# Loading q in rows of 1 KB and undoing the order where the outputs leave PSUM, in a retention and feed-forward kernel

## The chip, the cores and the metric

The kernel runs on one core of a Trainium2 chip. A core has a matrix engine (TensorE, PE in the profile) that writes its results to PSUM, eight banks of 512 fp32 values per partition; VectorE (DVE), ScalarE (ACT) and GpSimd (POOL) for elementwise work; SyncE (SP), which here issues transfers; and 16 DMA engines that carry them. PEld is TensorE's loading of weights. The metric is device time in microseconds (us) from the first to the last instruction. The kernel before takes 291.41 us, the median of three runs (291.38 to 291.48).

## What is computed

```python
# q, k, v: (8 batches, 8 heads, 576 tokens, 64), fp32
scores = scale * np.matmul(q, k.transpose(0, 1, 3, 2))
gamma = 1.0 - 2.0 ** (-5.0 - np.arange(H, dtype=np.float32))
Dmat = np.where(rel >= 0, gamma[:, None, None] ** rel[None, :, :], 0.0)   # rel = pos[:, None] - pos[None, :]
x = np.matmul(scores * Dmat[None], v)         # then heads side by side: (4608 tokens, 512)
h = np.maximum(x @ w_in, 0.0)                 # w_in: 512 x 2048
out = (h * h) @ w_out                         # w_out: 2048 x 512, out: (4608, 512) fp32
```

The first half is retention: attention without a softmax, with a decay per head. It can be computed in blocks of 64 tokens with a running state per head, and the kernel does so. The second half is a feed-forward layer with squared ReLU.

## The kernel before

The tokens are cut into 36 units: 32 "full" units of 128 tokens of one batch, and 4 "tail" units that join the last 64 tokens of two batches. The first 8 units go a way of their own ("paired"; not touched by the new load). Two units make a group, 18 in all. A unit's k, q and v are loaded as fp32, a partition per token, cast to fp16 by GpSimd (which also sorts the heads), and k and q are transposed by a DMA, so that the head dimension lies on the partitions. TensorE then forms, in quarters of its array (64 x 64, "quads"), the scores (psc), the sums of k and v for the state (psS) and the outputs (psO). VectorE masks the scores into rT, updates the state, and multiplies the outputs by powers of gamma while it moves them into xT, the input of the feed-forward matmuls ph (x by w_in) and po (by w_out; from the third group on, the second one in Strassen's seven products, whose sums are gS).

The order of instructions on each engine is not written down. Tasks with a modelled duration in us are handed to a list scheduler, and the program is emitted in the order that its simulation gives.

Loads, casts and transposes:

```python
    def dma_task(key, dur, fn, **kw):
        t = add("SP", key, dur, fn, deps=list(last_load), **kw)
        last_load[:] = [t]
        return t
# ...
    def add_load(u):
        kind, b, c = units[u]
        for n, (name, src) in enumerate((("k", k), ("q", q), ("v", v))):
            def fn(name=name, src=src):
                x = ld.tile([P, H, D], FP32, name=f"{name}32", tag=f"{name}32")
                tile_of[name + "32", u] = x
                if kind == "full":
                    nc.sync.dma_start(out=x, in_=src[b, :, c * P:(c + 1) * P, :].rearrange("h p d -> p h d"))
                else:
                    for i in range(2):
                        nc.sync.dma_start(out=x[i * 64:(i + 1) * 64],
                                          in_=src[b + i, :, 512:576, :].rearrange("h p d -> p h d"))
            loaded[name, u] = dma_task(0, 1.2 if loaded else 2.1, fn, acq=("ld",) if n == 0 else ())
# ...
        def sorted_cast(op, out_, in_):
            op(out=out_.rearrange("p (n b a d) -> p n b a d", n=2, b=2, a=2),
               in_=in_.rearrange("p (n a b) d -> p n b a d", n=2, a=2))

        def fk():
            t = tile_of["kq", u] = cast.tile([P, 2, H * D], FP16, name="kq16", tag="kq16")
            sorted_cast(nc.gpsimd.tensor_copy, t[:, 0], tile_of["k32", u])

        def fq():
            sorted_cast(nc.gpsimd.tensor_copy, tile_of["kq", u][:, 1], tile_of["q32", u])
# ...
        ck = add("POOL", base, 0.65, fk, deps=[loaded["k", u]], acq=("kq",))
        cq = add("POOL", base + 1, 0.62, fq, deps=[loaded["q", u], ck])
        cv = add("POOL", base + 2, 1.1, fv, deps=[loaded["v", u]] + tail, acq=("v16",))
# ...
        def fx2():
            t = tile_of["kqT", u] = work.tile([P, 2 * NP, P], FP16, name="kqT", tag="kqT", bufs=6)
            nc.sync.dma_start_transpose(out=t, in_=tile_of["kq", u].rearrange("p x n -> p (x n)"))
        T["kqT", u] = [add("SP", -1, 2.7, fx2, deps=[ck, cq], acq=("kqT",), after=3.0, lag=LAG_T)]
```

Here a row of q that a transfer moves is one token of one head, 64 fp32 values or 256 B. Scores, and the products of q with the state:

```python
    def emit_scores(g):

        tile_of["psc", g] = banks("psc")
        for s, u in enumerate(units_of(g)):
            kT = tile_of["kqT", u]
            ps = [x[:, cols(s)].rearrange("p (n i) -> p n i", i=64) for x in tile_of["psc", g]]
            for hp in range(NP):
                for a, c in ((0, 0), (1, 1), (0, 1), (1, 0)):
                    quad(ps[a][half(c), hp, :], kT[half(a), hp, half(c)], kT[half(a), NP + hp, half(c)], a, c)
# ...
    def put(g, u, c, h, lhsT, rhs, row):
        col = h % 2
        s = units_of(g).index(u)
        quad(tile_of["psO", g][c][half(col), 256 * s + 64 * (h // 2):256 * s + 64 * (h // 2) + 64], lhsT, rhs, row, col,
             start=(g, c, col) not in begun)
        begun.add((g, c, col))

    def inter(g, u, other):
        st = states(u)
        for n in range(2):
            for a, b in ((0, 0), (1, 1), (0, 1), (1, 0)):
                c = a ^ other
                if c in st:
                    x = 2 * n + b
                    put(g, u, c, 4 * n + 2 * a + b, tile_of[st[c][:2]][half(a), st[c][2], half(x)],
                        tile_of["kqT", u][half(a), NP + x, half(c)], a)

# ...
```

The masks, the eviction of the scores and the eviction of the outputs (add takes engine, priority, modelled us, what to emit; "ff" are the eight PSUM banks):

```python
    mask = const.tile([P, 64], FP32, name="mask")
    nc.gpsimd.memset(mask, 1.0)
    for c in range(2):
        nc.gpsimd.affine_select(out=mask[c * 64:(c + 1) * 64], in_=mask[c * 64:(c + 1) * 64],
                                compare_op=ALU.is_ge, fill=0.0, base=0, pattern=[[1, 64]], channel_multiplier=-1)
# ...
    def after_scores(g, t, key):
        for a in range(2):
            def fm(a=a):
                if a == 0:
                    tile_of["rT", g] = work.tile([P, 2, 2, NP, 64], FP16, name="rT", tag="rT", bufs=2)
                tile_of["masking", g] = nc.vector.tensor_tensor(
                    out=tile_of["rT", g][:, :, a],
                    in0=tile_of["psc", g][a].rearrange("p (s n i) -> p s n i", s=2, i=64),
                    in1=mask.rearrange("p (o r i) -> p o r i", o=1, r=1).to_broadcast([P, 2, NP, 64]), op=ALU.mult)
            m = add("DVE", key + a, 0.7, fm, deps=[t] + (T["masked", g][-1:] if a else []), acq=() if a else ("rT",))
            sched.free("ff", [m])
            T.setdefault(("masked", g), []).append(m)
        sched.free("prS", [m])
# ...
        for c in range(2):
            def fx(c=c):
                if c == 0:
                    tile_of["x", g] = x_pool.tile([P, NP, n * P], FP16, name="xT", tag="xT")
                nc.vector.tensor_tensor(
                    out=tile_of["x", g].rearrange("p n (s c i) -> p c s n i", s=n, c=2)[:, c],
                    in0=tile_of["psO", g][c].rearrange("p (s n i) -> p s n i", s=n, i=64),
                    in1=gam[units[us[0]][0]][:, c].rearrange("p (s n) i -> p s n i", s=1).to_broadcast([P, n, NP, 64]), op=ALU.mult)
            x = add("DVE", key + 0.1 * c, 0.7, fx, deps=[t2] + ([x] if c else []), acq=() if c else ("x",))
            sched.free("ff", [x])
        for u in us:
            T["x", u] = x
        sched.free("prO", [x])
```

The score matmuls of the next group and the output matmuls of the current one are emitted together from group 7 on.

## Time and profile before

| | us | share of the span |
|---|---|---|
| span of the profiled execution | 289.7 | |
| TensorE busy | 281.1 | 97% |
| ScalarE busy | 188.7 | 65% |
| VectorE busy | 181.2 | 63% |
| GpSimd busy | 85.8 | 30% |
| hardware DMA queue of SyncE: 134,848 packets, 44.84 MB | | 74.2% of 16 engines |

The profile is one execution. In its first part each engine's busy time is given; in the second the span is cut into 40 slices, and a digit is the busy share of a slice in tenths (9 is 90% or more). A row of the costliest groups names the line of the kernel, the engine, the operation, what it writes and reads ("out<-in"), then the shapes (partitions x elements and type), the count, the busy time in us and the mean ns of one instruction, and last the idle time of the engine just before these instructions with what ended it. A row of DMA issues gives the issuing engine's queue (SPq), the count, KB each, and the us from issue to landing. Matmuls are pipelined, so the durations of single ones overlap, and the end of a matmul is modelled.

### The profile page before, as it was taken

To read this page: it belongs to the slowest core of one execution; us is meant where nothing else is said; L and a number is where in the kernel's file an instruction comes from. 1 tells how busy PE (TensorE), PEld (TensorE's weight loads), DVE (VectorE), ACT (ScalarE), POOL (GpSimd) and SP (SyncE) were. 2 spreads that over 40 slices of the span, in tenths; PEclk is the share of its full clock that TensorE was granted. 3 is DMA by queue.
4 is the path that set the end of the run, shared out by engine and by line. 5 is a ranking of instruction groups with operands and counts; after the bars stand their busy time and mean duration, and the time that the engine had idled before them with its cause. 6 is when DMAs were issued, how large, how long until landed. Compare 5 with 4: busy or idle time off the path is not lost.

```text
span 289.7 us, 9992 instructions
## 1 busy us (share of the span) xinstructions
PE 281.1 (97%) x4322; PEld 233.3 (81%) x4322; DVE 181.2 (63%) x381; ACT 188.7 (65%) x361; POOL 85.8 (30%) x121
## 2 busy tenths in 40 slices
PE   7899999998999999999999999999999999999994
PEld 2568755787888888888888888888888888888883
DVE  3772369668585758736866757675777675455632
ACT  6459964684767676767767657586767676747830
POOL 5660035444434342342605151506240500000000
PEclk9999999999999999999999999999999999999998
DMA  7999999999899799999759699999994820201004
GB/s 197 276 208 205 249 289 256 183 228 210 186 185 211 158 225 198 214 223 231 149 147 211 139 226 198 180 190 211 226 179 140 186 83 2 75 2 72 2 6 141
DMA packets 139436, 49.94 MB, mean 172 GB/s; under 512 B 118144, under 2 KB 135040, under 8 KB 139392
## 3 DMA queue, kind: packets, MB, share of 16 engines
q1 hardware_dynamic: 134848, 44.84, 74.2%
q0 software_dynamic: 4224, 4.19, 8.8%
q8 instruction: 34, 0.56, 0.8%
q10 hardware_dynamic: 320, 0.26, 0.4%
q14 instruction: 10, 0.08, 0.1%
HBM read 36.70 MB, written 9.44 MB: 159 GB/s over the span
## 4 chain that ended last, share of the span: by engine, by line
PE 75%; DVE 1%; issue 0%; DVEq 0%
PE ph L853 36%; PE po L945 33%; PE psO L346 3%; PE psS L346 1%; PE psc L346 1%; DVE o L968 0%; DVE rT L673 0%; DVE p L997 0%; DVEq L968 0%
## 5 line engine op out<-in xcount | busy, mean ns | idle before, releaser
L853 PE MATMUL ph<-xT,w_in 128*128 128x256 f16 x1152 | 139.7, 273 | 0.1
L853 PEld LDWEIGHTS <-w_in 128*128 128x128 f16 x1152 | 110.9, 98 | 14.8 <-DMA w_in<-in_moe_w_in_dram 0.4
L861 ACT ACTIVATE rl<-ph 128x512 f16<-128x512 f32 x144 | 84.6, 588 | 49.6 <-PE ph L853 48.0
L871 ACT ACTIVATE gT<-rl 128x512 f16<-128x512 f16 x118 | 74.4, 631 | 3.4
L945 PEld LDWEIGHTS <-gS 128*128 128x128 f16 x512 | 49.5, 98 | 6.0
L945 PE MATMUL po<-wT,gS 128*128 128x256 f16 x384 | 51.9, 273 | 0.0
L922 DVE TENSOR_TENSOR gS<-gT,gS 128x512 f16<-128x512 f16 x64 | 32.5, 513 | 15.1 <-ACT gT L871 14.5
L945 PEld LDWEIGHTS <-gT 128*128 128x128 f16 x384 | 37.2, 98 | 5.3 <-issue 0.9
L922 DVE TENSOR_TENSOR gS<-gT 128x512 f16<-128x512 f16 x64 | 30.4, 477 | 15.7 <-ACT gT L871 15.6
L360 POOL CAST kq<-k 128x512 f16<-128x512 f32 x28 | 19.0, 679 | 63.8 <-DMA k<-in_k_dram 59.8
L945 PE MATMUL po<-w_out,gT 128*128 128x256 f16 x256 | 34.7, 273 | 0.7 <-DVE rT L673 0.7
L372 POOL TENSOR_TENSOR v<-v,vdec_full 128x512 f16<-128x512 f32 x24 | 26.6, 1107 | 20.2 <-DMA v<-in_v_dram 16.9
L360 POOL CAST kq<-q 128x512 f16<-128x512 f32 x28 | 18.5, 661 | 29.9 <-DMA q<-in_q_dram 29.7
L958 ACT COPY u<-po 128x256 f32<-128x256 f32 x32 | 11.8, 368 | 19.8 <-PE po L945 19.7
L968 DVE TENSOR_TENSOR o<-po,u 128x256 f32<-128x256 f32 x31 | 13.0, 420 | 16.0 <-PE po L945 9.3
L729 DVE TENSOR_TENSOR xT<-psO,gam_full 128x512 f16<-128x512 f32 x28 | 18.1, 685 | 6.5 <-PE psO L346 6.4
L873 DVE TENSOR_TENSOR gT<-rl 128x512 f16<-128x512 f16 x26 | 13.4, 517 | 12.4 <-ACT rl L861 11.9
L673 DVE TENSOR_TENSOR rT<-psc,mask 128x512 f16<-128x512 f32 x28 | 18.3, 683 | 3.4 <-PE psc L346 3.4
L968 DVE TENSOR_TENSOR o<-po,p 128x256 f32<-128x256 f32 x17 | 7.2, 423 | 16.7 <-ACT u L958 10.9
L945 PE MATMUL po<-w_out,gS 128*128 128x256 f16 x128 | 17.3, 273 | 0.0
L945 PE MATMUL po<-wT,gT 128*128 128x256 f16 x128 | 16.6, 273 | 0.0
L893 PE MATMUL po<-w_out,gT 128*128 128x512 f16 x64 | 15.8, 380 | 0.0
(78 smaller groups left out, 220.8 us busy)
## 6 DMA issues: line engine op xcount, KB each, us to landing
out_dram<-o SPq DMA_DIRECT2D x32, 256.0 KB, 3.5
k<-in_k_dram SPq DMA_DIRECT2D x24, 256.0 KB, 4.5
q<-in_q_dram SPq DMA_DIRECT2D x24, 256.0 KB, 5.1
v<-in_v_dram SPq DMA_DIRECT2D x24, 256.0 KB, 4.9
pair<-in_k_dram SPq DMA_DIRECT2D x4, 512.0 KB, 7.0
pair<-in_q_dram SPq DMA_DIRECT2D x4, 512.0 KB, 7.3
pair<-in_v_dram SPq DMA_DIRECT2D x4, 512.0 KB, 7.1
w_in<-in_moe_w_in_dram POOLq DMA_DIRECT2D x4, 512.0 KB, 8.9
```

The source lines that it names most:

```text
L346: t = nc.tensor.matmul(out_, lhsT=lhsT, rhs=rhs, start=start, stop=True, skip_group_check=True, tile_position=(64 * row, 64 * col))
L360: op(out=out_.rearrange("p (n b a d) -> p n b a d", n=2, b=2, a=2), in_=in_.rearrange("p (n a b) d -> p n b a d", n=2, a=2))
L372: nc.gpsimd.tensor_tensor(out=t, in0=tile_of["v32", u], in1=vdec[kind].rearrange("p (h o) -> p h o", o=1).to_broadcast([P, H, D]), op=ALU. ...
L673: tile_of["masking", g] = nc.vector.tensor_tensor(out=tile_of["rT", g][:, :, a], in0=tile_of["psc", g][a].rearrange("p (s n i) -> p s n i" ...
L729: nc.vector.tensor_tensor(out=tile_of["x", g].rearrange("p n (s c i) -> p c s n i", s=n, c=2)[:, c], in0=tile_of["psO", g][c].rearrange("p ...
L853: nc.tensor.matmul(tile_of["ph", g, fb][:, j, :], lhsT=w_in16[:, m, fi * P:(fi + 1) * P], rhs=tile_of["x", g][:, m, :], start=(m == 0), st ...
L861: nc.scalar.activation(out=t, in_=tile_of["ph", g, fb], func=ACTF.Relu)
L871: nc.scalar.activation(out=t, in_=rl, func=ACTF.Square)
L893: nc.tensor.matmul(tile_of["po", u], lhsT=tile_of["g", g][:, fi, s * P:(s + 1) * P], rhs=w_out16[:, fi, :], start=(fi == 0), stop=(fi == N ...
L922: nc.vector.tensor_tensor(out=Sx(k, h), in0=in0(h), in1=in1(h), op=op)
L945: nc.tensor.matmul(tile_of["pb", g, bank], lhsT=left(i), rhs=right[:, i, :], start=(start and i == 0), stop=(i == HF - 1), skip_group_chec ...
L968: nc.vector.tensor_tensor(out=o_tile(u)[:, half * HM:(half + 1) * HM], in0=bank(x), in1=tile_of[name, g], op=ALU.add)
```

## The change

A load of q for a full unit becomes four transfers, one for each x of 0 to 3 (the place of a head in its half of the eight heads); partition 32x + r holds, for the heads 4a + x of both halves a, the four consecutive tokens 4r to 4r + 3. Four tokens of one head lie next to each other in memory, so a row is 1 KB instead of 256 B, and there are a quarter as many rows. The price is a permuted q: after the cast and the transpose, the 64 columns of a block come in the order (t, r) with token 4r + t. Scores and products with the state keep that order, and TensorE reads q for them in four runs of 16 columns. The mask of full units has the same order. The eviction of the outputs puts it right: it reads PSUM with a step of 16 and writes xT in the order of tokens, in one multiply per unit and bank (four of 256 elements) instead of one per bank (two of 512). Heads are numbered 4a + 2n + b instead of 4n + 2a + b everywhere, so that both orders of loading agree. The two masks are kept in fp16. The scheduler's durations follow: 0.8 for a load of q, 0.43 for an eviction.

```diff
@@ -193,18 +193,20 @@
         make_vdec(f"pair{e}", iota_pair[:, e:e + 1])
 
 
-    heads = [(4 * n + 2 * a + b, n, a, b) for n in range(2) for a in range(2) for b in range(2)]
+    heads = [(4 * a + 2 * n + b, n, a, b) for n in range(2) for a in range(2) for b in range(2)]
     lncol = const.tile([P, NP], FP32, name="lncol")
     lnrow_R = const.tile([P, NP], FP32, name="lnrow_R")
     for h, n, a, b in heads:
-        nc.vector.memset(lncol[64 * b:64 * b + 64, 2 * n + a:2 * n + a + 1], lng[h])
+        nc.vector.memset(lncol[64 * b:64 * b + 64, h // 2:h // 2 + 1], lng[h])
         nc.vector.memset(lnrow_R[64 * a:64 * a + 64, 2 * n + b:2 * n + b + 1], lng[h])
 
-    mask = const.tile([P, 64], FP32, name="mask")
-    nc.gpsimd.memset(mask, 1.0)
-    for c in range(2):
-        nc.gpsimd.affine_select(out=mask[c * 64:(c + 1) * 64], in_=mask[c * 64:(c + 1) * 64],
-                                compare_op=ALU.is_ge, fill=0.0, base=0, pattern=[[1, 64]], channel_multiplier=-1)
+    mask = {}
+    for kind, pattern in (("tail", [[1, 64]]), ("full", [[1, 4], [4, 16]])):
+        m = mask[kind] = const.tile([P, 64], FP16, name=f"mask_{kind}")
+        nc.gpsimd.memset(m, 1.0)
+        for c in range(2):
+            nc.gpsimd.affine_select(out=m[c * 64:(c + 1) * 64], in_=m[c * 64:(c + 1) * 64],
+                                    compare_op=ALU.is_ge, fill=0.0, base=0, pattern=pattern, channel_multiplier=-1)
 
     mask2 = const.tile([P, 2, 2, 64], FP32, name="mask2")
     nc.gpsimd.memset(mask2, 1.0)
@@ -226,6 +226,7 @@
     EARLY = 20
     SQ_ACT = (0, 1, 2, 3, 4, 5, 6)
     SPREAD = 0.1
+    QL = 0.8
     SQ_LATE = (1, 4, 6)
     JOIN = 7
     LAG = {"k4": 0.7, "q4": 0.5}
@@ -286,13 +287,17 @@
             def fn(name=name, src=src):
                 x = ld.tile([P, H, D], FP32, name=f"{name}32", tag=f"{name}32")
                 tile_of[name + "32", u] = x
-                if kind == "full":
+                if kind == "full" and name == "q":
+                    for j in range(NP):
+                        nc.sync.dma_start(out=x[32 * j:32 * j + 32].rearrange("r (a t) d -> r a (t d)", a=2),
+                                          in_=src[b, :, c * P:(c + 1) * P, :].rearrange("(a x) (r t) d -> x r a (t d)", a=2, t=4)[j])
+                elif kind == "full":
                     nc.sync.dma_start(out=x, in_=src[b, :, c * P:(c + 1) * P, :].rearrange("h p d -> p h d"))
                 else:
                     for i in range(2):
                         nc.sync.dma_start(out=x[i * 64:(i + 1) * 64],
                                           in_=src[b + i, :, 512:576, :].rearrange("h p d -> p h d"))
-            loaded[name, u] = dma_task(0, 1.2 if loaded else 2.1, fn, acq=("ld",) if n == 0 else ())
+            loaded[name, u] = dma_task(0, QL if name == "q" and kind == "full" else 1.2, fn, acq=("ld",) if n == 0 else ())
 
     def add_load_pair(name, u):
         n = "kqv".index(name)
@@ -358,14 +363,18 @@
 
         def sorted_cast(op, out_, in_):
             op(out=out_.rearrange("p (n b a d) -> p n b a d", n=2, b=2, a=2),
-               in_=in_.rearrange("p (n a b) d -> p n b a d", n=2, a=2))
+               in_=in_.rearrange("p (a n b) d -> p n b a d", n=2, a=2))
 
         def fk():
             t = tile_of["kq", u] = cast.tile([P, 2, H * D], FP16, name="kq16", tag="kq16")
             sorted_cast(nc.gpsimd.tensor_copy, t[:, 0], tile_of["k32", u])
 
         def fq():
-            sorted_cast(nc.gpsimd.tensor_copy, tile_of["kq", u][:, 1], tile_of["q32", u])
+            if kind == "tail":
+                sorted_cast(nc.gpsimd.tensor_copy, tile_of["kq", u][:, 1], tile_of["q32", u])
+            else:
+                nc.gpsimd.tensor_copy(out=tile_of["kq", u][:, 1].rearrange("p (t a d) -> p a t d", t=4, a=2),
+                                      in_=tile_of["q32", u].rearrange("p (a t) d -> p a t d", a=2))
 
         def fv():
             t = tile_of["v16", u] = cast.tile([P, H, D], FP16, name="v16", tag="v16")
@@ -589,15 +598,19 @@
         g, s = place_of[units[u]]
         return {1: ("Rm", g, s), 0: ("R", g - 1, s)} if c else {1: ("Rm", g, s)}
 
+    def qT(u, a, x, c):
+
+        t = tile_of["kqT", u][half(a), NP:]
+        return t[:, x, half(c)] if units[u][0] == "tail" else t[:, :, 32 * x + 16 * c:32 * x + 16 * c + 16]
+
     def emit_scores(g):
 
         tile_of["psc", g] = banks("psc")
         for s, u in enumerate(units_of(g)):
-            kT = tile_of["kqT", u]
             ps = [x[:, cols(s)].rearrange("p (n i) -> p n i", i=64) for x in tile_of["psc", g]]
             for hp in range(NP):
                 for a, c in ((0, 0), (1, 1), (0, 1), (1, 0)):
-                    quad(ps[a][half(c), hp, :], kT[half(a), hp, half(c)], kT[half(a), NP + hp, half(c)], a, c)
+                    quad(ps[a][half(c), hp, :], tile_of["kqT", u][half(a), hp, half(c)], qT(u, a, hp, c), a, c)
 
     def emit_sums(g):
 
@@ -673,7 +686,7 @@
                 tile_of["masking", g] = nc.vector.tensor_tensor(
                     out=tile_of["rT", g][:, :, a],
                     in0=tile_of["psc", g][a].rearrange("p (s n i) -> p s n i", s=2, i=64),
-                    in1=mask.rearrange("p (o r i) -> p o r i", o=1, r=1).to_broadcast([P, 2, NP, 64]), op=ALU.mult)
+                    in1=mask[units[units_of(g)[0]][0]].rearrange("p (o r i) -> p o r i", o=1, r=1).to_broadcast([P, 2, NP, 64]), op=ALU.mult)
             m = add("DVE", key + a, 0.7, fm, deps=[t] + (T["masked", g][-1:] if a else []), acq=() if a else ("rT",))
             sched.free("ff", [m])
             T.setdefault(("masked", g), []).append(m)
@@ -722,15 +735,20 @@
                 elif at == 0:
                     sched.free("Rm", [t2, T["Rmread", rg]])
         sched.free("rT", [t2])
+        x = None
+        full = units[us[0]][0] == "full"
         for c in range(2):
-            def fx(c=c):
-                if c == 0:
-                    tile_of["x", g] = x_pool.tile([P, NP, n * P], FP16, name="xT", tag="xT")
-                nc.vector.tensor_tensor(
-                    out=tile_of["x", g].rearrange("p n (s c i) -> p c s n i", s=n, c=2)[:, c],
-                    in0=tile_of["psO", g][c].rearrange("p (s n i) -> p s n i", s=n, i=64),
-                    in1=gam[units[us[0]][0]][:, c].rearrange("p (s n) i -> p s n i", s=1).to_broadcast([P, n, NP, 64]), op=ALU.mult)
-            x = add("DVE", key + 0.1 * c, 0.7, fx, deps=[t2] + ([x] if c else []), acq=() if c else ("x",))
+            for at, u in enumerate(us):
+                def fx(c=c, at=at):
+                    if ("x", g) not in tile_of:
+                        tile_of["x", g] = x_pool.tile([P, NP, n * P], FP16, name="xT", tag="xT")
+                    at_ = at * P + 64 * c
+                    y = tile_of["psO", g][c][:, cols(at)]
+                    nc.vector.tensor_tensor(
+                        out=tile_of["x", g][:, :, at_:at_ + 64].rearrange("p n (r t) -> p n r t", t=4),
+                        in0=y.rearrange("p (n t r) -> p n r t", n=NP, t=4) if full else y.rearrange("p (n r t) -> p n r t", n=NP, t=4),
+                        in1=gam_f[:, :, 64 * c * full:64 * c * full + 64].rearrange("p n (r t) -> p n r t", t=4), op=ALU.mult)
+                x = add("DVE", key + 0.1 * (2 * c + at), 0.43, fx, deps=[t2] + ([x] if x else []), acq=() if x else ("x",))
             sched.free("ff", [x])
         for u in us:
             T["x", u] = x
# (left out: the same renumbering of heads in the paired units, in the sums for the state and in the index of rT)
```

More of the change, by code (lines that the diff above doesn't have):

```diff
@@ L218 @@
         nc.scalar.activation(out=gam_f[:, hp, :], in_=iota_f, func=ACTF.Exp, scale=lncol[:, hp:hp + 1])
-    gam = {"full": gam_f.rearrange("p n (c i) -> p c n i", c=2),
-           "tail": gam_f[:, :, 0:64].rearrange("p n (c i) -> p c n i", c=1).to_broadcast([P, 2, NP, 64])}
     dec128 = const.tile([P, NP], FP32, name="dec128")
@@ L409, in fc @@
                         engines[eng](out=t.rearrange("p (n b a d) -> p n b a d", n=2, b=2, a=2),
-                                     in_=x.rearrange("p (n a b) d -> p n b a d", n=2, a=2))
+                                     in_=x.rearrange("p (a n b) d -> p n b a d", n=2, a=2))
                 dur = (dict(POOL=1.1, DVE=0.6) if name == "v" else dict(POOL=0.62, DVE=0.4, ACT=0.59))[eng]
@@ L487, in fk @@
                     for s, a in ((0, 0), (1, 1), (0, 1), (1, 0)):
-                        h = 4 * (hp // 2) + 2 * a + hp % 2
+                        h = 4 * a + hp
                         quad(ps[s][half(a), 64 * hp:64 * hp + 64], tile_of["kx", u][half(s), e, 128 * hp + 64 * a:128 * hp + 64 * a + 64],
@@ L526, in inter @@
                         x = 2 * n + b
-                        put2(s, 4 * n + 2 * a + b, before(s)[half(a), half(x)], kqT(s)[half(a), NP + x, :], a)
+                        put2(s, 4 * a + x, before(s)[half(a), half(x)], kqT(s)[half(a), NP + x, :], a)
         def put2(s, h, lhsT, rhs, row):
@@ L542, in fo1 @@
                         put2(s, h, tile_of["vx", u][half(s), e, 64 * h:64 * h + 64],
-                             rT[e][half(s), m % 2, 2 * (m // 2) + b, :], s)
+                             rT[e][half(s), m // 2, 2 * (m % 2) + b, :], s)
         def fo2():
@@ L612, in emit_sums @@
                 for c, a in ((0, 0), (1, 1), (0, 1), (1, 0)):
-                    h = 4 * (hp // 2) + 2 * a + hp % 2
+                    h = 4 * a + hp
                     quad(ps[c][half(a), hp, :], tile_of["kq", u][half(c), 0, half(2 * hp + a)],
@@ L634, in inter @@
                     x = 2 * n + b
-                    put(g, u, c, 4 * n + 2 * a + b, tile_of[st[c][:2]][half(a), st[c][2], half(x)],
-                        tile_of["kqT", u][half(a), NP + x, half(c)], a)
+                    put(g, u, c, 4 * a + x, tile_of[st[c][:2]][half(a), st[c][2], half(x)],
+                        qT(u, a, x, c), a)
     def emit_out1(g):
@@ L648, in emit_out2 @@
                     put(g, u, c, h, tile_of["v16", u][half(c), h, :],
-                        tile_of["rT", g][half(c), s, m % 2, 2 * (m // 2) + b, :], c)
+                        tile_of["rT", g][half(c), s, m // 2, 2 * (m % 2) + b, :], c)
             inter(g, u, 0)
```

## The prediction

> **What bounds the kernel now.** I read the engine shares and the slices first.
>
> ```profile
> PE 281.1 (97%) x4322; PEld 233.3 (81%) x4322; DVE 181.2 (63%) x381; ACT 188.7 (65%) x361; POOL 85.8 (30%) x121
> ...
> DMA  7999999999899799999759699999994820201004
> ```
>
> TensorE is busy for 281.1 of 289.7 us. Next to it the DMA engines are almost full until about two thirds of the span and then nearly empty. So there are two candidates for the bound, and busy time does not say which one holds the end. The table of busy time by stretch does, here for everything between the start-up and the last results:
>
> ```profile
> core 0: us, PE busy (x) PEld busy (x) DVE busy (x) ACT busy (x) POOL busy (x), PEclk, DMA share, GB/s
> 20.00:285.00 265.00, 263.63 (x4070) 223.94 (x4068) 166.69 (x327) 178.97 (x341) 72.83 (x90) 1.00 0.83 169
> ```
>
> In 265 us TensorE is idle for 265.00 - 263.63 = 1.37 us, at full clock. The view of who waited for whom says who pays for the full DMA queue:
>
> ```profile
> POOL kq L360 <- DMA k<-in_k_dram: 59.8, 16, 9.4
> ...
> POOL kq L360 <- DMA q<-in_q_dram: 29.7, 20, 6.7
> ...
> DVE xT L729 <- PE psO L346: 6.4, 8, 1.4
> ...
> PE po L945 <- DVE rT L673: 0.7, 1, 0.7
> ```
>
> Columns: total us, times, longest us. GpSimd waits for loads of k and q for 89.5 us in all. No line has TensorE waiting for GpSimd, a load or a transpose in the steady part: the casts run far enough ahead that a late load is swallowed. TensorE's own largest steady wait is 0.7 us, once, for a VectorE eviction. Thus TensorE's instruction stream is the bound, and the loads are hidden.
>
> [...] its packet records give 22 ns on average for the 256 B packets of the hardware queue and 66 ns for 1 KB packets (the packets of the output stores in that size), so 1 KB in four packets costs 88 ns and in one 66 ns.
>
> [...] The new moving operand of the score matmuls comes in runs of 16 fp16 values, 32 B[...]. No matmul of this trace reads such runs[...].
>
> [...] the new PSUM read is by VectorE, with a step of 16 fp32 values (64 B). No instruction of this trace reads PSUM so. The nearest is the paired eviction, which reads PSUM contiguously but reads its factor and writes its output with a step of two, and takes 728 ns against 685.
>
> **The change part by part.** These are the rows by shape and the DMA issues that I use:
>
> ```profile
> L673 DVE TENSOR_TENSOR rT<-psc,mask 128x512 f16<-128x512 f32 x28 | 18.3, 683 | 3.4 <-PE psc L346 3.4
> L729 DVE TENSOR_TENSOR xT<-psO,gam_full 128x512 f16<-128x512 f32 x28 | 18.1, 685 | 6.5 <-PE psO L346 6.4
> ...
> L968 DVE TENSOR_TENSOR o<-po,u 128x256 f32<-128x256 f32 x31 | 13.0, 420 | 16.0 <-PE po L945 9.3 <-ACT u L958 6.5
> ...
> L562 DVE TENSOR_TENSOR xT<-psO,gam_full 128x512 f16<-128x512 f32 x8 | 5.4, 728 | 3.3 <-PE psO L346 3.3
> ```
>
> ```profile
> k<-in_k_dram SPq DMA_DIRECT2D x24, 256.0 KB, 4.5
> q<-in_q_dram SPq DMA_DIRECT2D x24, 256.0 KB, 5.1
> ```
>
> *Loads of q (24 full units after the paired ones).* 1,024 packets of 256 B become 256 of 1 KB. Spread over 16 engines that is 1,024 x 22 / 16 = 1.41 us before and 256 x 66 / 16 = 1.06 us after, 0.35 us less per unit and about 8.4 us of transfer time in all. It lies beside TensorE and shortens only GpSimd's waits. On the path: 0.
>
> *Issue of those loads.* SyncE issues four transfers where it issued one. The shortest issue in its timeline is 0.36 us (an output store) and the median of a q issue 0.92 us, so four would be 1.4 us at least: some 0.5 us more per unit, 12 us over the kernel. SyncE is busy issuing for 184 us (the sum over its timeline), nearly all of that before 233 us, so it has some 20% of room. On the path: 0.
>
> *Casts.* GpSimd's cast of q moves the same 512 elements in the same runs of 64; I leave it at 661 ns. 0.
>
> *Start.* GpSimd builds two masks instead of one: one more memset (152 ns) and two more selects (236 ns each, overlapped), about 0.7 us. In the timeline its constants end at 4.88 us, and VectorE's small instruction behind them at 5.14, directly ahead of the first cast of k at 5.13. That cast would start at about 5.8. But the load of the first q lands only at 6.9, and TensorE's transposes of q start at 7.42 behind it, so most of the 0.7 us falls into that wait. I put 0.1 us on the path, as an estimate from these times.
>
> *Scores and state products on TensorE.* 24 units x 16 score quads, and 336 state products (16 per unit, 8 where the chain of a batch begins: 18 x 16 + 6 x 8), read q through the new pattern, 720 quads. Their number and their columns stay. In the timeline 32 score quads take 0.43 us of which 0.19 is the length of the last one, so 7.5 ns each. If runs of 32 B are free, 0.
>
> *Evictions.* In 14 groups two multiplies of 512 become four of 256. Consecutive 512-element multiplies start 0.61 us apart in VectorE's timeline, two together took 1.28 us. By the 420 ns row, less the same overlap of some 75 ns, four take 4 x 0.345 + 0.075 = 1.45 us. So 0.17 us more per group, 2.4 us of VectorE in all, which goes from 63% to 64%. What counts is how long before its first use the input of the feed-forward part is ready. From the timeline, comparing the end of the second eviction with the first matmul that reads it: 0.48 us in the tightest group (eviction 121.31 to 122.59, matmul at 123.07), then 1.42, 1.68, 2.35 and 3.0 us, and over 4 us in most others. 0.17 us fits into all of them. On the path: 0. The 512-element row of the mask product (683 ns) does not change by a half-width mask[...].
>
> *Emission order.* The kernel orders its instructions by a model with the new durations (0.43 for an eviction, 0.8 for a q load), so the order of everything after the paired units can move. The one steady wait of 0.7 us, at 65 us, may go or another may appear. I take half of it, -0.3 us, plus and minus 0.7.
>
> Sum: 0.1 + 0 - 0.3 + about 0.1 for evictions that fall badly = -0.1 us. 291.4 - 0.1 = 291.3 us.
>
> **The rivals.**
>
> *The strided moving operand is slow.* If 32 B runs halved the rate at which TensorE reads q, 720 quads would each take another 7.5 ns: +5.4 us, all on the bound, 296.8 us. [...] for it, that no trace has tried it. I give it 5%.
>
> *The strided PSUM read is slow.* [...] That makes +1 to +2 us: about 292.8. For it: the step of 64 B[...]. Against it: the step of two in the paired evictions costs only 43 ns. I give it 25%.
>
> *SyncE becomes the bound of the loads.* If each of four issues took the median 0.9 us, a unit would cost SyncE 2.7 us more, 5.4 per group of about 14.5 us, with 20% (2.9 us) of room. Then transposes come later from group to group. The transposed tiles are made some 5 us before their use (a transpose issued at 161.74, landing in about 4.3 us, and its scores at 172.6), so this would reach TensorE only after several groups: up to +3 us. Short transfers of a quarter of the packets speak against it. 7%.
>
> *Loads were the hidden bound.* If the shorter loads freed something, TensorE could gain at most its 1.37 us of steady idle, so 290.0 us. Nothing can make this kernel 2% (5.8 us) faster: its idle is 289.7 - 281.1 = 8.6 us, and 7.2 us of that is start and end, which the q loads of later units do not touch.
>
> **Range and chances.** From 290.5 (all of the steady wait gone) to 292.9 (slow PSUM reads), middle 291.3. Faster by over 2% would need shorter matmuls: 0.01. Slower by over 2% needs the slow moving operand or a starving SyncE together with something else: 0.03. Within 2%: 0.96.
>
> **What would show it.** In the changed profile: DMA share and packets under 512 B fall (by 24,576), GpSimd's wait for q shrinks, and TensorE's busy time stays at 281 us within 1 us. The eviction row shows 56 instructions of about 420 ns[...]. The score quads' sections stay at 0.43 us for 32; 0.67 would be the slow operand. SyncE's issues of q near 0.4 us each; near 0.9 would be the third rival. I would be wrong most simply if a new wait of TensorE for a VectorE or ScalarE eviction shows up because of the new order.

## The result

| | us, median (runs) | ratio to the kernel before, 95% interval |
|---|---|---|
| before | 291.39 (291.28 to 291.48, 4) | |
| changed | 293.12 (292.76 to 293.69, 4) | 1.0061 [1.0044, 1.0079] |
| predicted | 291.3, range 290.5 to 292.9 | |

The change costs 1.7 us, and the result lies 0.2 us above the range. The loads became cheaper as planned, the evictions and the permuted tiles cost what was predicted, and yet TensorE stands still for longer. The changed kernel's engine shares and its DMA slices, which answer to the first lines shown of before:

```profile
PE 281.8 (96%) x4322; PEld 233.4 (80%) x4322; DVE 185.2 (63%) x409; ACT 187.9 (64%) x361; POOL 84.8 (29%) x124
...
DMA  7999999998898898999969698979788310201004
```

TensorE's busy time is 281.8 us where it was 281.1, in a span of 292.0 where it was 289.7: the work is the same, the idle time grew from 8.6 to 10.2 us. By stretch (busy us of each engine between 20 and 287 us):

```profile
20.00:287.00 267.00, 264.04 (x4067) 223.65 (x4065) 170.59 (x354) 178.38 (x341) 71.16 (x90) 1.00 0.78 168
```

The steady part has 2.96 us of idle TensorE instead of 1.37. The waits (total us, times, longest us) name the larger half of the difference:

```profile
POOL kq L365 <- DMA k<-in_k_dram: 52.6, 20, 7.1
POOL kq L376 <- DMA q<-in_q_dram: 26.9, 22, 4.4
...
PE po L963 <- DVE rT L686: 1.7, 1, 1.7
...
PE ph L871 <- issue: 0.3, 1, 0.3
```

GpSimd waits less for k and q than before (52.6 and 26.9 us instead of 59.8 and 29.7). The one steady wait of 0.7 us, for the eviction rT at 65 us, has become 1.7 us, and there is a new pause of 0.3 us in which TensorE waits for nothing that the page shows ("issue"). The rows that the prediction named:

```profile
L747 DVE TENSOR_TENSOR xT<-psO,gam_full 128x256 f16<-128x256 f32 x56 | 20.2, 417 | 6.7 <-PE psO L351 6.6
...
q<-in_q_dram SPq DMA_DIRECT2D x96, 64.0 KB, 3.5
```

56 evictions take 417 ns each, no longer than a contiguous PSUM read of 256 elements before (o<-po,u, 420 ns) in spite of their step of 64 B, and a q transfer lands 3.5 us after its issue instead of 5.1. What remains is the third thing that the change does, the planner's numbers, above all the time assumed for a load of q (0.8 instead of 1.2 us). TensorE's program of the changed kernel has the same instructions in the same order as before up to row 3302 (a load of weights and a product are a row each, 8,644 in all, numbered from 2 behind two records of TensorE's sequencer), near 114 us. Behind it, 866 rows stand elsewhere (by the names of the tiles that they write and read).

### The profile page after: what moved, and what is told of

Read it like the earlier page. It is cut to its first block, busy times and chain, and to the rows that moved or that the text cites. A ratio compares the mean times of both kernels' runs of the same rounds, so it can differ in the third digit from the quotient of the medians.

```text
span 292.0 us, 10140 instructions
## 1 busy us (share of the span) xinstructions
PE 281.8 (96%) x4322; PEld 233.4 (80%) x4322; DVE 185.2 (63%) x409; ACT 187.9 (64%) x361; POOL 84.8 (29%) x124
## 4 chain that ended last, share of the span: by engine, by line
PE 75%; DVE 1%; issue 0%; DVEq 0%
PE ph L871 36%; PE po L963 33%; PE psO L351 3%; PE psS L351 1%; PE psc L351 1%; DVE rT L686 0%; DVE o L986 0%; DVE p L1015 0%; DVEq L986 0%
## 5 line engine op out<-in xcount | busy, mean ns | idle before, releaser
L940 DVE TENSOR_TENSOR gS<-gT,gS 128x512 f16<-128x512 f16 x64 | 33.6, 524 | 21.5 <-ACT gT L889 20.8
L940 DVE TENSOR_TENSOR gS<-gT 128x512 f16<-128x512 f16 x64 | 33.1, 519 | 14.2 <-ACT gT L889 14.0
L365 POOL CAST kq<-k 128x512 f16<-128x512 f32 x28 | 18.4, 657 | 53.8 <-DMA k<-in_k_dram 52.6
L381 POOL TENSOR_TENSOR v<-v,vdec_full 128x512 f16<-128x512 f32 x24 | 25.8, 1074 | 27.6 <-DMA v<-in_v_dram 23.9
L747 DVE TENSOR_TENSOR xT<-psO,gam_full 128x256 f16<-128x256 f32 x56 | 20.2, 417 | 6.7 <-PE psO L351 6.6
L376 POOL CAST kq<-q 128x512 f16<-128x512 f32 x24 | 15.5, 645 | 27.0 <-DMA q<-in_q_dram 26.9
L891 DVE TENSOR_TENSOR gT<-rl 128x512 f16<-128x512 f16 x26 | 12.4, 478 | 13.2 <-ACT rl L879 12.8
L686 DVE TENSOR_TENSOR rT<-psc,mask_full 128x512 f16<-128x512 f32 x24 | 16.1, 683 | 1.7 <-PE psc L351 1.6
```

Source lines behind the costliest of these rows:

```text
L376: nc.gpsimd.tensor_copy(out=tile_of["kq", u][:, 1].rearrange("p (t a d) -> p a t d", t=4, a=2), in_=tile_of["q32", u].rearrange("p (a t) d ...
L381: nc.gpsimd.tensor_tensor(out=t, in0=tile_of["v32", u], in1=vdec[kind].rearrange("p (h o) -> p h o", o=1).to_broadcast([P, H, D]), op=ALU. ...
L686: tile_of["masking", g] = nc.vector.tensor_tensor(out=tile_of["rT", g][:, :, a], in0=tile_of["psc", g][a].rearrange("p (s n i) -> p s n i" ...
L747: nc.vector.tensor_tensor(out=tile_of["x", g][:, :, at_:at_ + 64].rearrange("p n (r t) -> p n r t", t=4), in0=y.rearrange("p (n t r) -> p ...
L940: nc.vector.tensor_tensor(out=Sx(k, h), in0=in0(h), in1=in1(h), op=op)
```

## The experiments

Each was timed against runs of the kernel before on the same chip (median 291.86 to 291.91 us in the four groups of runs; 291.39 in the runs of the result above). The letters of the theories are those of each group: in the first group (the first four kernels), A is the data path, with loads that move GpSimd's casts onto VectorE's products; from the second group on, A is the new sequence.

**The cause at 65 us: e1.** In the changed kernel's timeline VectorE's float16 products and sums (gT and gS, called products below) are long just where GpSimd casts k and q or multiplies v:

```profile
62.70 0.61 POOL L365 CAST kq<-k 128x512 f16<-128x512 f32 x1 [7.06 <-DMA k<-in_k_dram]
62.71 0.88 DVE L891 TENSOR_TENSOR gT<-rl 128x512 f16<-128x512 f16 x1 [0.54 <-ACT rl L879]
...
63.63 0.88 DVE L940 TENSOR_TENSOR gS<-gT,gS 128x512 f16<-128x512 f16 x1
...
64.35 1.06 POOL L381 TENSOR_TENSOR v<-v,vdec_full 128x512 f16<-128x512 f32 x1
...
64.43 1.26 DVE L940 TENSOR_TENSOR gS<-gT 128x512 f16<-128x512 f16 x1
...
66.36 0.68 DVE L686 TENSOR_TENSOR rT<-psc,mask_full 128x512 f16<-128x512 f32 x1
...
67.09 0.49 PE L963 MATMUL po<-w_out,gT 128*128 128x256 f16 x3 [1.72 <-DVE rT L686]
```

Columns: start, us, engine. A product of two SBUF operands took 420 ns where GpSimd was idle (103 of them in this trace, 406 to 426 ns) and up to 1,267 beside GpSimd. rT, which frees a PSUM bank for the next product, comes behind them, and TensorE waits. Why GpSimd's work stretches a product beside it no trace shows; that it does, e9 shows below (0.41 to 0.43 us each at this place, once GpSimd's cast comes later). The first experiment shortens GpSimd's casts of units 10 and 11; it leaves out seven of eight heads of these units (filled with zeros).

```diff
+    SHORT = (10, 11)
-            sorted_cast(nc.gpsimd.tensor_copy, t[:, 0], tile_of["k32", u])
+            if u in SHORT:
+                nc.gpsimd.tensor_copy(out=t[:, 0, 0:D], in_=tile_of["k32", u][:, 0])
+                nc.gpsimd.memset(t[:, 0, D:], 0.0)
+            else:
+                sorted_cast(nc.gpsimd.tensor_copy, t[:, 0], tile_of["k32", u])   # q and v likewise
```

> The changed kernel, but GpSimd's casts of units 10 and 11 read one head of eight and fill the rest with zeros (part of the computation is left out; the order of all instructions on the other engines is the same). Theory A: the changed kernel's wait of TensorE at 65 us (1.72 us, for VectorE's masking of the scores) comes from GpSimd's casts of these two units, which overlap VectorE's fp16 sums and stretch them from 0.42 to 0.88-1.26 us. Then those sums take 0.42-0.45 us, the wait falls under 0.5 us and the time falls by 1.2 to 1.7 us, to about 291.6. Rival B: VectorE is late there because of the new evictions or the order. Then the sums stay long or the wait stays, and the time stays at 293.1.

Measured: 291.61 us, ratio 0.9985 [0.9970, 1.0000]. The products at 62 to 64 us take 0.42 to 0.52 us and the pause at 65 us is gone, as theory A said. The profile, of the slowest of the 12 runs, has a larger pause at 131 us (1,227 ns from one start to the next, where 109 is normal) and one at 170 us, so in this execution part of the gain was given back.

**The second mask: e2.** The first product of the feed-forward part began at 17.99 us instead of 17.74. This kernel builds the masks behind GpSimd's other constants.

```diff
-    mask = {}
-    for kind, pattern in (("tail", [[1, 64]]), ("full", [[1, 4], [4, 16]])):   # ahead of mask2
+    # the same lines, at the end of make_tail_pool, behind iota_pt
```

> The changed kernel, with the building of both score masks moved behind GpSimd's small constants for the tail, so that VectorE's first cast of k is not held; all else is the same. Theory A: the second mask at the start delays the first feed-forward matmul from 17.74 to 17.99 us; then it starts at 17.75 or earlier and the time falls by 0.2 to 0.4 us, to about 292.8. Rival B: the later start comes from the landing of the first loads; then it stays at 18.0 and the time at 293.1.

Measured: 292.72 us, 1.0022 [1.0012, 1.0032]; first product at 17.73 us. The fifth run below shows 17.74 with the mask left where it was, so the 0.25 us of the first profile came and went without the mask being moved.

**The old sequence: e3.** The planner's numbers are set so that TensorE's and ScalarE's sequences are those of before, row by row; loads, layouts, masks and evictions stay as changed.

```diff
-    QL = 0.8
+    QL = 1.2
-                x = add("DVE", key + 0.1 * (2 * c + at), 0.43, fx, ...)
+                x = add("DVE", key + 0.1 * (c + at / 2), 0.35, fx, ...)
```

> The changed kernel with the scheduler's durations of the kernel before (1.2 for a load of q, two times 0.35 for the pair of evictions that replaces one): TensorE, ScalarE and VectorE get their instructions in the order of the kernel before, only with four evictions for two. Theory A: the loss at 65 us stays, since both kernels have the same order there, and about 1.0 us that was lost after 110 us comes back: about 292.1. Rival B: the order makes no difference and the loss after 110 us is from the transfers or evictions: 293.1. Rival C: the whole loss is order: 291.4.

Measured: 291.76 us, 0.9995 [0.9983, 1.0006], as rival C had it. The whole change except its sequence costs nothing, and gains nothing.

**Four q loads alone: e4.** The kernel before, with a q load as four transfers of 32 partitions in rows of 256 B.

```diff
-                if kind == "full":
+                if kind == "full" and name == "q":
+                    for j in range(NP):
+                        nc.sync.dma_start(out=x[32 * j:32 * j + 32],
+                                          in_=src[b, :, c * P + 32 * j:c * P + 32 * j + 32, :].rearrange("h p d -> p h d"))
+                elif kind == "full":
```

> The kernel before, with each load of q for a full unit issued as four transfers of 32 partitions in rows of 256 B as before; orders and everything else the same. Theory A: the four issues alone hold back the loads behind them on SyncE, the k of unit 10 lands later than 61.2 us, GpSimd's casts move into VectorE's sums and TensorE's wait at 65 us grows from 0.71 to about 1.7 us: about 292.4 us. Rival B: the shape of the rows or the permuted reading does it; then the time stays at 291.4.

Measured: 290.64 us (5 runs), 0.9961 [0.9948, 0.9974]. Four issues don't enlarge the pause at 65 us: in this profile there is none. q came 1.6 us later (its cast starts at 63.92 us instead of 62.31, behind most of the products), and the products take 0.42 to 0.43 us. So what the loads do to this pause depends on when they land.

**The changed kernel once more: e5.** No edit.

> The changed kernel once more, unaltered, as the measure for the three beside it on the same chip. Both theories: 1.0044 to 1.0079 of the kernel before, some 1.2 to 2.3 us over it, as when it was first timed; its profile has a pause of TensorE between rows 4018 and 4022 of its instructions (599 ns from start to start in the first profile).

Measured: 292.53 us (291.06 to 293.60, 17 runs), 1.0014 [1.0001, 1.0027]: still over the kernel before, by less than at first. The intervals of the two measurements don't meet. The size of the loss thus depends on the executions; what can be told apart from here on is told by pairs of one group, and by several kernels.

**The new sequence in the old kernel: e6.** One number of the kernel before.

```diff
-            loaded[name, u] = dma_task(0, 1.2 if loaded else 2.1, fn, ...)
+            loaded[name, u] = dma_task(0, 0.8 if name == "q" and kind == "full" else 1.2, fn, ...)
```

> The kernel before with one number of its planner changed: the time it assumes for the load of a full q tile, 0.8 in place of 1.2 us. Loads, layouts, casts, masks and evictions are those of before; the sequences of TensorE and ScalarE are those of the changed kernel. Theory A (the new sequence costs the time): over the kernel before by 0.8 to 1.8 us, ratio 1.003 to 1.006, and the pause at row 4018 is there. Theory B (the data path costs it: four q loads, four evictions, the late mask): within 0.4 us of the kernel before, ratio 0.9985 to 1.0015, no pause there.

Measured: 293.73 us (293.44 to 294.08, 5 runs), 1.0059 [1.0046, 1.0072]. Nothing of the data path changed, and the time is 1.8 us longer. TensorE's steady waits (total us, times, longest us), where before has only the first, of 0.7 us:

```profile
PE po L945 <- DVE rT L673: 0.8, 1, 0.8
PE ph L853 <- DMA w_in<-in_moe_w_in_dram: 0.2, 1, 0.2
PE ph L853 <- DVE rT L673: 0.2, 1, 0.2
PE po L945 <- DVE gS L922: 0.2, 1, 0.2
```

With e3 this is the answer to the main question: the loss is that of the sequence.

**The old estimate in the changed kernel: e7.** QL = 1.2, nothing else. TensorE's sequence is that of before but for 120 rows, which the planner's numbers for the evictions move (counted as the 866).

> The changed kernel with that number put back to 1.2, all else as changed. Theory A: back to the kernel before, ratio 0.998 to 1.002, with no pause at row 4018. Theory B: as the changed kernel, 1.0044 to 1.0079.

Measured: 291.93 us, 1.0000 [0.9991, 1.0009]. Its profile even has a longer pause at 65 us (1,465 ns from start to start; before 987), and it is level all the same. On this chip the new sequence thus costs 0.6 us with the new data path (e5 against e7, whose intervals overlap) and 1.8 with the old one (e6). In the first group it is 1.0 with the new data path (e2 against e3, apart from the mask; their intervals don't meet).

**The pause near row 4020: e8.** In the chain of waits of the changed kernel (start, us, what) it comes behind 160 rows of 64 x 64 products, which TensorE went through in 0.8 us:

```profile
132.15 0.37 PE psS L351 x32
132.53 0.40 PE psO L351 x48
132.93 0.43 PE ph L871 x3
133.36 0.33 issue
```

It lies between rows 4018 and 4020, the third and the fourth of four equal products on one input into one bank, so no tile is new there. The page lists a queue that brings instructions:

```profile
q8 instruction: 34, 0.56, 0.8%
```

These are 34 packets of 16 KB. TensorE's 8,644 rows over 34 packets are 254 each; 256 rows to a packet (34 x 256 = 8,704) is an estimate from these numbers. If a new piece begins at the pause and the others lie 256 rows apart (a fit to the pause, not a record), the piece for it landed at 132.17 us, 1.52 us before TensorE went on at 133.69. In e1 these are 130.76 and 132.27, 1.51 us apart. (The 1.73 us of the expectation are counted to a record four rows on, row 4024.) So the theory: TensorE had run dry of instructions. The test moves the pieces against the work, by cutting five warm-up products into eight each.

```diff
+        parts = 8 if len(warmed) < 5 else 1
+        warmed.append(0)
+        w = 512 // parts
+        for i in range(parts):
+            nc.tensor.matmul(warm_ps[0][:, i * w:(i + 1) * w], lhsT=junk[:, 0:P], rhs=junk[:, i * w:(i + 1) * w], start=True, stop=True)
-        nc.tensor.matmul(warm_ps[0], lhsT=junk[:, 0:P], rhs=junk, start=True, stop=True)
```

> The changed kernel with the first five warm-up products of TensorE cut into eight pieces of 64 columns each: the same streaming in the warm-up, but 70 more instructions ahead of everything else, so that the ends of the 16 KB pieces in which TensorE's instructions arrive fall 70 rows earlier in the work. Theory A1 (the pause at row 4018 is TensorE waiting for its next piece of instructions: in the two profiles that have it, it ended 1.73 us after that piece had landed by the row count): no pause over 150 ns between rows 4088 and 4092 (the old 4018 to 4022), and 0.3 to 1.2 us less than the unaltered changed kernel. Theory A2 (it waits for a PSUM bank or for data): the pause stays, 0.3 to 1.2 us, and so does the time.

Measured: 292.15 us, 1.0007 [0.9997, 1.0017]. TensorE's timeline at the same work (start, us):

```profile
131.22 0.45 PE L356 MATMUL psS<-v,kq 64*64 64x64 f16 x32
...
131.81 0.25 PE L356 MATMUL psO<-kqT,R 64*64 64x64 f16 x8
131.99 2.47 PE L876 MATMUL ph<-xT,w_in 128*128 128x256 f16 x21
```

21 products in one run: the pause is gone. The time is 0.4 us under e5, with intervals that overlap. This fits theory A1, since the data and the banks at this place are the same. Two of the seven profiles of the unshifted sequence lack the pause too, so one profile doesn't settle it; the other two shifted kernels (e15, e16) lack it as well. What the pause is worth isn't shown by this pair.

**Held casts: e9 and e10.** One wait more in the kernel before, and in the changed kernel: GpSimd's cast of unit 10 waits for the first rT of group 4. No engine's sequence changes.

```diff
+            # where the first rT of group 4 is emitted
+            if g == 4 and a == 0:
+                behind(tile_of["kcast", 10], tile_of["masking", g])
```

> The kernel before with one wait added: GpSimd's cast of the k tile of unit 10 (61.24 us in the profile of before) waits for VectorE's first mask of scores of that step (rT, 65.09 us); no sequence of any engine changes. Theory C (the pause of TensorE at 65 us is VectorE's float16 products, 1.27 us instead of 0.42 beside a GpSimd cast, which hold back rT and with it a PSUM bank): VectorE's products at 62 to 65 us take 0.41 to 0.43 us each, rT starts near 64.1 us, the pause of 987 ns from start to start shrinks under 250 ns, and the time falls by 0.6 to 1.1 us, ratio 0.9962 to 0.998. Theory D (the pause comes from elsewhere, such as the product before or ScalarE): pause and time as before, within 0.3 us.

> The same wait in the changed kernel, in its own sequence. Theory C: no pause at 65 us (1988 and 1416 ns in two profiles of the changed kernel), 0.8 to 1.7 us less than the changed kernel, that is 0.999 to 1.002 of the kernel before; what stays over the kernel before with the same wait is the new sequence (pauses near 131 and 171 us), 0.5 to 1.5 us. Theory D: no change against the changed kernel.

Measured: e9 291.86 us, 0.9997 [0.9990, 1.0005]; e10 291.75 us, 0.9990 [0.9976, 1.0004]. The timeline of e9, at the place shown above:

```profile
62.69 0.43 DVE L878 TENSOR_TENSOR gT<-rl 128x512 f16<-128x512 f16 x1 [0.54 <-ACT rl L866]
...
63.16 0.42 DVE L927 TENSOR_TENSOR gS<-gT,gS 128x512 f16<-128x512 f16 x1
63.50 0.41 DVE L927 TENSOR_TENSOR gS<-gT 128x512 f16<-128x512 f16 x1
...
64.17 0.68 DVE L673 TENSOR_TENSOR rT<-psc,mask 128x512 f16<-128x512 f32 x1
...
64.97 0.61 POOL L360 CAST kq<-k 128x512 f16<-128x512 f32 x1 [10.11 <-DVE rT L673]
65.09 0.86 PEld L950 LDWEIGHTS <-gT 128*128 128x128 f16 x8
65.20 1.04 PE L950 MATMUL po<-w_out,gT 128*128 128x256 f16 x8
```

With GpSimd out of the way, the products take 0.42 us, rT comes at 64.17 us (65.09 before), and TensorE goes on without a pause. Theory C is right about the mechanism and wrong about the time: in e9 the pause of 0.87 us is gone and the median is where it was. Its profile lost 0.31 us between rows 1000 and 1400, 0.52 in four shorter stretches up to row 5005, and 0.3 behind the last product, against the first profile of before. Whether the held casts cause these isn't known. In e10 the gain against e5 (0.8 us, another chip) is within the reach of the intervals. Against e9, on the same chip, e10 should by theory C have been 0.5 to 1.5 us slower through its sequence; it is 0.1 us faster.

**Four loads again: e11.** The kernel of e4 (its label says held, the kernel has no held casts).

> The kernel before with the q loads as four transfers of 32 rows in the old layout, once more, on this chip. Theory C (its gain was the pause at 65 us, which its later q missed): 0.8 to 1.4 us under the kernel before, within 0.4 us of the kernel with held casts. Rival (four smaller transfers are better of themselves): over 0.5 us under the kernel with held casts.

Measured: 291.60 us (20 runs), 0.9986 [0.9977, 0.9996]: 0.3 us faster than before and not 1.2; 0.3 us under e9. The first measurement of it flattered, and neither theory's figure came.

**Old sequence, late mask and held casts: e12.**

> The changed kernel with TensorE's and ScalarE's sequences of before (the two planner estimates put back), the second mask built later, and the casts of unit 10 held as in the two runs above. If the changed data path costs nothing of itself: as the kernel before with held casts, 290.6 to 291.3 us, ratio 0.996 to 0.998. If the four evictions or the permuted tiles cost something that other pauses hid: over it by 0.4 us or more.

Measured: 291.17 us (290.90 to 291.54, 8 runs), 0.9971 [0.9959, 0.9983], the best of its group and faster than the kernel before. No part of it alone gave this gain (e3 0.9995, e9 0.9997), and it was timed in one group of 8 runs, as e4 was in one of 5; so where its 0.7 us come from, and whether they last, is not shown. It is 0.6 us under e10, which has the new sequence and the early mask on the same data path. Its only steady wait of TensorE:

```profile
PE ph L875 <- DMA w_in<-in_moe_w_in_dram: 0.2, 1, 0.2
```

**What the sequence's loss consists of: e13 to e16.** The kernel before unaltered; the kernel before with the new sequence and held casts (e14), and with the new sequence and the shifted stream (e16); the changed kernel with both (e15).

> The kernel before, unaltered, run as a kernel under test. If the comparison is sound: ratio 0.999 to 1.001. If neighbouring runs of one and the same program differ by 0.3 us or more in the median, then differences of that size between the other kernels mean nothing. Its profile should have the pause at 65 us (987 ns in the first); if it hasn't, that pause comes and goes in the kernel before too.

> The kernel before with the new sequence, 1.82 us over the kernel before on the last chip, and with the casts of unit 10 held until rT. If the wait at 65 us is the main part of what the sequence costs: 1 to 1.8 us less, ratio 1.000 to 1.003. If the pause near row 4020 and the waits near 171 us are: 0 to 0.9 us less, ratio 1.003 to 1.006.

> The changed kernel with held casts and with its instruction stream shifted by 70 rows. If the pause near row 4020 costs time in most executions: 0.3 to 0.6 us less than the changed kernel with held casts alone (0.999 of before), so 0.997 to 0.998. If it is made up for later: 0.9985 to 1.0005.

> The kernel before with the new sequence and the stream shifted by 70 rows. If the pause near row 4020 is the main part of what the sequence costs: 0.8 us or more less than the 1.82 us over the kernel before, ratio under 1.0035. If the bank waits are: 0 to 0.5 us less, ratio 1.004 to 1.006. In either case no pause between rows 4088 and 4092 of its profile.

Measured: e13 292.09 us, 1.0008 [0.9999, 1.0017]; e14 293.51, 1.0056 [1.0042, 1.0071]; e15 291.89, 0.9998 [0.9989, 1.0008]; e16 293.04, 1.0038 [1.0024, 1.0051]. A kernel against itself differs by 0.2 us, so such differences mean nothing here. The wait at 65 us is not what the sequence costs (e14). The shifted stream brings 0.7 us of 1.8 (e16; its interval and that of e6 overlap a little), less than the 0.8 and more than the 0.5 that would have decided for one cause. Against e14, on the same chip but with held casts, it is 0.5. In the changed kernel with held casts it brings nothing (e15); that profile has a new wait of 0.6 us for a sum gS, near 199 us.

All profiles in one table. "Path" is the data path, "sequence" the order of TensorE. The next three columns are us lost in a stretch of rows against the first profile of before, which itself lost 0.87 at 65 us (so -0.87 is no pause). The last is the time from the landing of the piece of instructions to TensorE's row 4024.

| run | path, sequence | ratio | rows 1700 to 2000 (65 us) | 3593 to 4069 (131 us) | 5005 to 5485 (170 us) | piece to row 4024, us |
|---|---|---|---|---|---|---|
| changed | new, new | 1.0061 | 1.00 | 0.49 | 0.29 | 1.73 |
| e5 | new, new | 1.0014 | 0.43 | 0.14 | 0.70 | 1.71 |
| e2 mask later | new, new | 1.0022 | 0.13 | 0.06 | 0.00 | 1.73 |
| e1 short casts | new, new | 0.9985 | -0.87 | 1.11 | 0.41 | 1.73 |
| e10 held | new, new | 0.9990 | -0.87 | 0.54 | 0.15 | 1.75 |
| e6 | old, new | 1.0059 | 0.09 | 0.32 | 0.71 | 1.63 |
| e14 held | old, new | 1.0056 | -0.87 | 0.87 | 0.75 | 1.63 |
| e8 shifted | new, new | 1.0007 | 0.09 | 0.00 | 0.00 | 2.03 |
| e15 held, shifted | new, new | 0.9998 | -0.87 | 0.11 | 0.00 | 1.88 |
| e16 shifted | old, new | 1.0038 | -0.05 | 0.00 | 0.45 | 2.29 |
| e3 | new, old | 0.9995 | -0.03 | 0.00 | 0.00 | 3.36 |
| e7 | new, old but 240 rows | 1.0000 | 0.48 | 0.01 | 0.00 | 2.77 |
| e12 held, mask later | new, old | 0.9971 | -0.87 | 0.00 | 0.00 | 2.53 |
| e13 | old, old | 1.0008 | 0.01 | 0.00 | 0.00 | 3.56 |
| e9 held | old, old | 0.9997 | -0.87 | 0.07 | 0.00 | 2.18 |
| e4 four loads | old, old | 0.9961 | -0.87 | 0.00 | 0.11 | 3.08 |
| e11 four loads | old, old | 0.9986 | -0.87 | 0.00 | 0.00 | 2.92 |

At 65 us TensorE's sequence is the same in every kernel, and the pause varies from none to 1.4 us in kernels with the old sequence and to 1.9 with the new. The other two belong to the sequence: at 131 us 0.06 to 1.11 us in all seven profiles that have the new one unshifted, at most 0.11 elsewhere; at 170 us 0 to 0.75 in the ten with the new sequence against at most 0.11. (Not all of the column for 131 us is the pause at row 4020: it is there in five of the seven and ended 1.41 to 1.54 us after the landing. In e2 and e5 TensorE stopped for 0.05 and 0.13 us at rows 3978 and 3982 instead, 0.88 us after it, and in e6 and e10 0.1 and 0.3 us went at row 3854. e15, with the stream shifted, has a stop of 0.1 us at row 3978 too, so this one isn't tied to the piece.) Where the pause at 65 us was taken away and the stream left, the loss at 131 us was the largest (e1, e14): in e14 TensorE reached row 3842 1.44 us earlier than in e6 (129.37 instead of 130.81), but the piece landed only 0.89 us earlier (130.70 instead of 131.59). That is one way in which a gain is given back.

At 170 us the same overlap as at 65 us shows. In e6:

```profile
167.71 1.04 POOL L372 TENSOR_TENSOR v<-v,vdec_full 128x512 f16<-128x512 f32 x1 [5.17 <-DMA v<-in_v_dram]
167.75 1.28 DVE L873 TENSOR_TENSOR gT<-rl 128x512 f16<-128x512 f16 x1 [0.53 <-ACT rl L861]
...
168.70 0.81 POOL L360 CAST kq<-k 128x512 f16<-128x512 f32 x1
...
169.84 0.61 PE L945 MATMUL po<-wT,gS 128*128 128x256 f16 x4 [0.18 <-DVE gS L922]
...
171.52 0.60 PE L853 MATMUL ph<-xT,w_in 128*128 128x256 f16 x4 [0.20 <-DVE rT L673]
```

VectorE's gT takes 1.28 us beside GpSimd's product for v, then TensorE waits for gS and for the bank that rT frees. This is read from the traces; no run held GpSimd here.

## Why the prediction was wrong

- **The step that failed** is the emission order: "may go or another may appear. I take half of it, -0.3 us, plus and minus 0.7." Two things were wrong in it. The sign: a change of the planner's estimate was counted as half a gain, on the one wait that the page showed, and that wait (row 1700 to 2000) lies where the sequence doesn't change at all. And the size: alone, in the kernel before, the new sequence cost 1.8 us (e6), and its removal from the changed kernel left the time of the kernel before (e3, e7). The prediction's last sentence named the event, a new wait through the new order (for an eviction, as at 170 us; the pause at 131 us is, by its fit, one for instructions), but gave it no place in the sum above +0.4. The upper end of the range came from slow PSUM reads instead, the author's estimate of a rate that no run shows; the sum with its own 0.7 us to either side would have given 290.6 to 292.0. The second measurement of the changed kernel (ratio 1.0014, e5) would lie within the range, but by luck: the cost is the sequence's there too.
- **The wait at 65 us.** The prediction read it as a wait for an eviction and didn't ask why the eviction was late. It was late because a product of VectorE took up to 1.27 us beside GpSimd's casts and its product for v (e9 shows the place without them); in the first profile of the changed kernel more of them did, and TensorE lost 1.0 us more. That is a matter of when the loads land and not of TensorE's sequence, and taking this pause away in e9 did not shorten the median.
- **Loads of q**: right, 0 on the path. Small packets fell by 23,424 (predicted 24,576; packets of 4 B, which grew by 1,152, make the difference), q lands in 3.5 us instead of 5.1, GpSimd waits less, and TensorE gains nothing (e3).
- **Issue**: right on the path (0), wrong in its size. The issues have a median of 427 ns each, but those of q add up to 62.9 us instead of 37.0, 26 us more and not 12. SyncE's total grew by only 7.3 us because its other issues became shorter (those of v 19.6 us instead of 29.0), which the prediction didn't foresee.
- **Start**: 0.25 us in the first profile, 0.00 in e5; the estimate of 0.1 is within that scatter.
- **Scores and state products**: right. 32 score quads take 0.43 us as before (0.43 to 0.51 us from 60 us on, in both kernels), with q read in runs of 32 B.
- **Evictions**: right. 417 ns, 0.335 us apart, four in 1.42 us in most groups (predicted 1.45). Of the inputs that they write, the tightest was ready 3.2 us ahead of its first use in the new sequence, and 0.35 us in the old one (e3), where it was 0.48 before: 0.13 us later, where 0.17 was predicted. (VectorE's share stays at 63%; the sum gives that too, not 64.) The mask product takes 683 ns with the float16 mask as with the old one, as predicted. The rival of slow PSUM reads, given 25%, did not come: 256 elements more cost 685 - 420 = 265 ns before, so at half the rate an eviction would have taken some 685 ns, by an estimate from these rows.
- **The other rivals**: no slow operand, no SyncE bound, no hidden load bound.

What stays open: how much of the sequence's 1.8 us each pause is worth. In e16, with the pause at 131 us gone, 1.15 us remain; its profile shows 0.45 us at 170 us and 0.4 us more behind the last product (4.95 us instead of 4.55, in e6, e14 and e16 alike, but not with the new data path), and no run changed these. Why the sequence costs 1.6 to 1.8 us with the old data path (e6, e14) and only 0.6 to 1.0 with the new one (e5 against e7, e10 against e12, e2 against e3), why the changed kernel lost 1.7 us at first and 0.6 in e5, and why held casts brought nothing in e9, is open too.

## What to carry to other kernels

A number in a planner that orders instructions is part of a change: time the kernel with the new data path and the old order, and the other way round, before either is judged. Where TensorE waits for an eviction, look at what delayed the eviction's engine; here float16 products of two SBUF operands on VectorE grew up to threefold (0.42 to 1.27 us) beside GpSimd's casts and products. The same kernel timed twice differed by 0.25% (e4, e11) and by 0.47% (the changed kernel, e5), so a profile's single pause of 0.9 us, which is 0.3%, need not show in the median when it is taken away.

## What the runs showed of the hardware

- Some pauses of TensorE fit a wait for its own instructions; no record names such a wait (in the changed kernel the profile has 0.33 us of "issue"). In a stretch where 256 of its rows took 4 us (8.6 us on average), it stood still in five of seven profiles of the new sequence until 1.41 to 1.54 us after a 16 KB piece had landed; with the piece's end moved by 70 rows, in none of three. In the old sequence the 256 rows up to row 4024 took 3.8 us, but the piece had landed 2.2 to 3.6 us ahead; what sets when a piece is fetched was not tried. If the pieces begin at row 4020 and every 256 rows from it, no piece's first row ran sooner than 1.39 us after its landing, in any profile after the first 20 us.
- VectorE read 256 elements of PSUM with a step of 64 B in 417 ns (xT<-psO in the changed kernel), and contiguously in 420 (o<-po,u before).
- 64 x 64 products whose moving operand lies in runs of 32 B took no longer than with contiguous ones: 0.43 us for 32 in both kernels.
- SyncE issued a load of q of 64 KB in 256 rows in 427 ns (median, changed kernel), one of 256 KB in 1,024 rows in 0.92 us (before). The loads of v, 256 KB in 1,024 rows in both kernels, took 1.00 us before and 0.43 in the changed kernel, so the size alone doesn't set it.
